# A head pair's attention handed to the scheduler in 16 stages instead of 8

## The chip, the core and the metric

The kernel runs on one core of a Trainium2 chip. The core has a matrix engine (TensorE, called PE in the profile, with its weight loads as PEld), a vector engine (VectorE, DVE), a scalar engine (ScalarE, ACT), GpSimd (POOL) and a queue that issues DMA transfers (SyncE, SP). Each engine works through its own instructions in the order of its queue and waits on semaphores for the others. The metric is the time of one execution on the device in microseconds (us); lower is better.

## The reference

The computation is a sliding-window attention followed by a feed-forward layer with softplus. There are 8 sequences of 576 tokens, 8 heads of 64 numbers each:

```python
scores = scale * np.matmul(q, k.transpose(0, 1, 3, 2))
mask = (rel >= 0) & (rel < window)              # window = 64
scores = np.where(mask, scores, -1000000000.0)
scores = scores - np.max(scores, axis=-1, keepdims=True)
attn = np.exp(scores)
attn = attn / (np.sum(attn, axis=-1, keepdims=True) + 1e-09)
x = np.matmul(attn, v)                          # then heads side by side: 4608 x 512
h = x @ w_in                                    # 512 x 2048
g = np.maximum(h, 0.0) + np.log1p(np.exp(-np.abs(h)))
out = g @ w_out                                 # 2048 x 512
```

All inputs are float32.

## The kernel before

**Blocks.** The 4608 tokens are cut into 12 blocks of 384. For each block the attention is computed for four head pairs, which gives x (512 rows by 384 tokens, as a high and a low part). Then come 16 steps of the feed-forward layer, one for each slice of 128 of the 2048 hidden columns. A step n consists of an *up* (12 matmuls into one bank of `ps_h`, line 396), a softplus, and a *down* (9 matmuls into the three banks of `ps_o`, line 417). Each product is taken in three passes, of high and low parts.

**Softplus.** For every step ScalarE reads the up's bank and takes the absolute value (line 400), the exponential (401) and the logarithm (402). VectorE reads the bank a last time and adds the maximum (404). A high part g0 is cast (406, on VectorE or ScalarE by turns) and a low part g1 subtracted (407, VectorE). The pool `ps_h` has two banks, so the up of step n+2 cannot start before line 404 of step n has run.

**Attention of a head pair** from the third block on: load q and k; split them into high and low parts (lines 242 to 247); three groups of score matmuls (262), each followed by a masked reading with row minimum on VectorE (269); the fold of the window (275); six exponentials (279); row sums and division (282 to 285); a split of the weights into three bf16 parts `nat` (304 to 311), which two transposing DMAs turn into `tr` (307, 312); a split of v (320 to 324); matmuls of `tr` with v (371), one group for each head; and the addition of the parts and the casts to x (376 to 380). The buffers `tr`, `nat`, `v_in`, `v12`, `v13`, `k0` and `k1` exist once.

**Order of the work.** `attention` is a generator; each `yield` ends a stage. Every stage, every up and every down is an event at a slot, and the events are emitted in the order of their slots:

```python
events.append((2 * n + 0.5, lambda g=g, f=f: ffn_up(g, f)))
events.append((2 * n + DOWN, lambda step=steps[n]: ffn_down(*step)))
```

With DOWN = 5.5 the down of step n stands behind the up of step n+2. A pair's stages stand at a base (8 slots apart from the next pair, so four feed-forward steps per pair) plus the numbers of `STG`; the third block has `BASE[2]` and `PACE[2]` for its base, and the table `STG2`. From slot 100 on (`PE_ORDERED_FROM`) TensorE keeps the order of the events. Before that slot on TensorE, and everywhere on the other engines, a scheduler orders the instructions of each engine by the order of emission and by a timeline of its own, so a stage's slot is a rank, not a time.

Of the kernel before, what the change touches and what calls it, by code (L numbers as in the profile page):

```python
# [8 lines left out]
F32 = mybir.dt.float32  # L9
BF16 = mybir.dt.bfloat16  # L10
F32R = mybir.dt.float32r
# [4 lines left out]
P = 128  # L16
TB = 384
# [3 lines left out]
CH = 64  # L21
NCH = TB // CH + 1
# [1 line left out]
SPLIT = 8  # L24
DOWN = 5.5
CONVERT = (-104, -98, -93, -88, -6, -3, 0, 3, 6, 8, 11, 13, 16, 18, 21, 24)
BASE = (-100, -10, 29)
PACE = (5, 4, 4.5)
STG0 = (-4.5, 0.5, 1, 2, 3, 4, 7, 8)
STG2 = (-6, -3, 0, 1, 2, 3, 12, 13)  # L30
STG = (-14, -8, 0, 1, 2, 3, 15, 17)
SH, SHP = -13, 8
PE_ORDERED_FROM = 100
MANUAL = {mybir.EngineType.PE}

# [4 lines left out]
def window_attention_softplus_ffn(  # L40
# [24 lines left out]
    nc = tc.nc  # L65
# [13 lines left out]
    att = ctx.enter_context(tc.tile_pool(name="att", bufs=1))  # L79
# [29 lines left out]
    W = CH + P  # L109
# [72 lines left out]
    def attention(g, hp):  # L182
        c0 = hp * P
        t0 = ORDER[g] * TB
        prev = t0 % S != 0
        by_pe = g < 2
        odd0 = g == 0 and hp % 2 == 1

        def bank():
            if not odd0:  # L190
                return ps_a.tile([P, 512], F32, name="ps_a")

            taken_ps[0] += 1
            return ps_o.tile([P, 512], F32, name=f"ps_o{taken_ps[0] % NJ}")

        heads = [slice(0, D), slice(D, P)]
# [9 lines left out]
        else:  # L206
            q_in = ld.tile([P, 2, TB], F32, name="q_in")
            k_in = ld.tile([P, 2, W - P + TB], F32, name="k_in")
            ts, ks = slice(t0, t0 + TB), slice(t0 - CH, t0 + TB)
# [9 lines left out]
        if by_pe:  # L219
            v_pad = v_pads[hp % 2]  # L220

            def load_v(rows, lay, j0, start):
                n = rows.stop - rows.start
                for j in range(j0, NJ):
                    dst = v_pad[rows, lay, j, :, :].rearrange("p h (i d) -> p (h i) d", i=2)[:, 0:4:3, :]
                    s = start + j * P
                    nc.sync.dma_start(dst, v[s : s + n, c0 : c0 + P].rearrange("p (h d) -> p h d", h=2))

            if t0 == 0:
                dst = v_pad[CH:P, 0, 0, :, :].rearrange("p h (i d) -> p (h i) d", i=2)[:, 0:4:3, :]  # L230
                nc.sync.dma_start(dst, v[0:CH, c0 : c0 + P].rearrange("p (h d) -> p h d", h=2))
            load_v(slice(0, P), 0, 1 if t0 == 0 else 0, t0 - CH)
            load_v(slice(0, CH), 1, 0, t0 + CH)
            load_v(slice(CH, P), 1, 0, t0)
        else:
            v_in = att.tile([P, NCH, P], F32, name="v_in")
            for half in heads:
                nc.sync.dma_start(v_in[half, :, :], v[ks, c0 : c0 + P].rearrange("(c p) n -> p c n", p=CH))
            q_hl = att.tile([P, 2, TB], F32R, name="q_hl")
            k_hi, k_lo = [att.tile([P, 2, W - P + TB], F32R, name=f"k{i}") for i in range(2)]  # L240
            low = heads[1]
            nc.scalar.copy(q_hl, q_in)  # L242
            nc.scalar.copy(k_hi, k_in)  # L243
            nc.vector.tensor_tensor(  # L244
                q_hl[low, :, :], q_in[low, :, :], q_hl[low, :, :].bitcast(F32), ALU.subtract
            )
            nc.vector.tensor_tensor(k_lo, k_in, k_hi.bitcast(F32), ALU.subtract)
        yield

# [26 lines left out]
        for hh in range(2):  # L276
            for j in range(NJ):
                i = hh * NJ + j
                nc.scalar.activation(  # L279
                    sv[:, i, 0:P], sv[:, i, 0:P], AF.Exp, bias=mn[:, hh, j : j + 1], scale=-1.0, accum_out=sm[:, i : i + 1]  # L280
                )
        nc.vector.tensor_scalar(sm, sm, 1.0e-9, None, ALU.add)
        nc.vector.reciprocal(sm, sm)
        pn = sv[:, :, 0:P]
        nc.vector.tensor_tensor(pn, pn, sm.unsqueeze(2).to_broadcast([P, 2 * NJ, P]), ALU.mult)  # L285
        if by_pe:

            pt = att.tile([P, 2, TB], F32, name="pt", tag="q_hl")
            for hh in range(2):
                pp = bank()  # L290
                for j in range(NJ):
                    tp(pp[:, j * P : (j + 1) * P], sv[:, hh * NJ + j, 0:P], ident)
                (nc.vector.tensor_copy if hh else nc.scalar.copy)(pt[:, hh, :], pp[:, :TB])
        else:

            nat = att.tile([P, 2, 4 * NJ, 2, CH], BF16, name="nat")
            tr = att.tile([P, 8 * NJ, P], BF16, name="tr")
            pv = [pn.rearrange("p i (f c) -> p i f c", f=2), nat.rearrange("p s (i f) b c -> p s i f b c", f=2)]

            def part(s, b):  # L300
                return pv[1][:, s, :, :, b, :]

            n = 4 * NJ
            nc.scalar.copy(part(0, 0), pv[0])
            nc.vector.tensor_tensor(pv[0], pv[0], part(0, 0), ALU.subtract)
            nc.scalar.copy(part(0, 1), pv[0])  # L306
            nc.sync.dma_start(
                tr[:, 0:n, :], nat[:, 0, :, :, :].rearrange("p n b c -> p (n b c)"), transpose=True
            )
            nc.vector.tensor_tensor(part(1, 0), pv[0], part(0, 1), ALU.subtract)  # L310
            nc.vector.tensor_copy(nat[:, 1, :, 1, :], nat[:, 0, :, 0, :])
            nc.sync.dma_start(
                tr[:, n:, :], nat[:, 1, :, :, :].rearrange("p n b c -> p (n b c)"), transpose=True
            )

            v12 = att.tile([P, NCH, 2, 2, D], BF16, name="v12")
            v13 = att.tile([P, NCH, 2, D], BF16, name="v13")
            vv = v_in.rearrange("p c (h d) -> p c h d", h=2)
            up, low = heads
            nc.scalar.copy(v12[:, :, :, 0, :], vv)  # L320
            nc.vector.tensor_tensor(vv, vv, v12[:, :, :, 0, :], ALU.subtract)  # L321
            nc.scalar.copy(v12[:, :, :, 1, :], vv)  # L322
            nc.vector.tensor_tensor(v13[low, :, :, :], vv[low, :, :, :], v12[low, :, :, 1, :], ALU.subtract)
            nc.vector.tensor_copy(v13[up, :, :, :], v12[up, :, :, 0, :])
# [13 lines left out]
        for hh in range(2):  # L338
# [14 lines left out]
            for s in range(2):  # L353
                for c in range(0 if prev else 1, NCH):
# [3 lines left out]
                    n = s * 4 * NJ + (hh * NJ + j) * 2  # L358
# [6 lines left out]
                    else:  # L365
                        at = n * P + CH
# [83 lines left out]
    for g in range(NB):  # L450
        for hp in range(NP):
            if g < 3:
                base = BASE[g] + PACE[g] * hp
            else:
                base = 2 * NF * (g - 1) + SHP * hp + SH
            stages = attention(g, hp)
            for at in STG if g >= 3 else STG2 if g >= 2 else STG0:
                events.append((base + at, lambda stages=stages: next(stages, None)))
    loaded = 0
    for n, (g, f, first, last) in enumerate(steps):  # L460
# [57 lines left out]
```

## Time and profile before

| | |
|---|---|
| Runs of the kernel before | 1089.43 us median of 3 (1089.07 to 1093.37) |
| The profiled execution's own time | 1091.76 us |
| Its span, first to last instruction | 1090.0 us |
| TensorE busy | 1011.9 us, 93% |
| VectorE busy | 826.5 us, 76% |
| ScalarE busy | 743.1 us, 68% |
| Mean granted TensorE clock | 0.977 |

The span has three parts: until about 137 us the first two blocks' attention and the preparation of the weights; then the feed-forward steps together with the attention of later blocks, until about 958 us; then the last steps without attention. Rows of the timeline read: start in us, duration in us, engine, line, operation, output and inputs, count of merged instructions, and in brackets the idle time before it with the engine that ended it.

### The profile page before, as it was taken

What the parts mean: (1) busy time and instruction counts of PE and PEld (TensorE: products, weight loads), DVE (VectorE), ACT (ScalarE), POOL (GpSimd) and SP (SyncE); (2) the same over time, 40 slices, a digit from 0 to 9 for tenths busy, and PEclk for the clock granted to TensorE, in tenths of its full rate; (3) what the DMA queues carried; (4) which work ended last, traced back from release to release, by engine and by line L of the source; (5) the groups of instructions that cost most, each with busy time, mean ns of one, the idle gap of its engine ahead of it and who ended that gap; (6) DMA issues with size and microseconds to landing.
All of it is one profiled execution on the core that took longest, in us unless ns stands there. A gap on an engine that the chain in (4) does not pass through costs nothing.

```text
span 1090.0 us, 16756 instructions
## 1 busy us (share of the span) xinstructions
PE 1011.9 (93%) x5888; PEld 882.7 (81%) x5888; DVE 826.5 (76%) x1797; ACT 743.1 (68%) x1705; POOL 53.4 (5%) x53
## 2 busy tenths in 40 slices
PE   5879689999999999999999999999999999999998
PEld 3667588887888888888887888888888888888897
DVE  7799897687878777887788778878877877875332
ACT  4466487776876776776777677667767766775433
POOL 3233420000000000000000000000000000000000
PEclk8889789999999999999999999999999999999999
DMA  6575254465645443543444344434535743521000
GB/s 196 159 248 186 80 144 111 92 144 99 161 92 117 107 102 78 136 125 79 121 111 108 107 107 122 111 83 113 143 78 95 156 89 79 143 57 29 29 1 30
DMA packets 209750, 119.07 MB, mean 109 GB/s; under 512 B 143361, under 2 KB 201729, under 8 KB 208129
## 3 DMA queue, kind: packets, MB, share of 16 engines
q1 hardware_dynamic: 209664, 118.00, 43.4%
q8 instruction: 46, 0.75, 0.3%
q14 instruction: 40, 0.32, 0.1%
HBM read 76.28 MB, written 10.22 MB: 79 GB/s over the span
## 4 chain that ended last, share of the span: by engine, by line
PE 58%; ACT 17%; DVE 16%; DMA 4%; issue 3%; SPq 1%; ACTq 0%
PE ps_h L396 25%; PE ps_o L417 23%; ACT st L279 6%; PE ps_a L371 6%; PE ps_a L262 4%; DVE st L285 3%; DVE v_in L321 3%; ACT k L243 2%; ACT q_hl L242 2%; DVE st L269 2%; DVE u L404 2%; ACT u L400 1%; ACT v L322 1%; ACT u L401 1%; ACT x L379 1%
## 5 line engine op out<-in xcount | busy, mean ns | idle before, releaser
L396 PE MATMUL ps_h<-x,w 128*128 128x384 f32 x2304 | 454.2, 345 | 41.6 <-DVE u L404 40.9
L396 PEld LDWEIGHTS ps_h<-x,w 128*128 128x128 f32 x2304 | 404.6, 190 | 69.2 <-DVE u L404 56.5
L417 PE MATMUL ps_o<-w,g 128*128 128x512 f32 x1728 | 433.3, 394 | 0.7 <-DVE g L407 0.7
L417 PEld LDWEIGHTS ps_o<-w,g 128*128 128x128 f32 x1728 | 316.7, 188 | 57.7 <-DVE g L407 1.1
L400 ACT ACTIVATE u<-ps_h 128x384 f32<-128x384 f32 x192 | 93.5, 487 | 143.0 <-PE ps_h L396 126.6
L404 DVE SCALAR_TENSOR_TENSOR u<-ps_h,u 128x384 f32<-128x384 f32 x192 | 106.1, 553 | 77.0 <-ACT u L402 76.0
L407 DVE TENSOR_TENSOR g<-u,g 128x384 fp32r<-128x384 f32 x192 | 105.6, 550 | 24.2 <-ACT g L406 22.6
L279 ACT ACTIVATE st<-st,mn 128x128 f32<-128x128 f32 x288 | 111.5, 391 | 14.1 <-DVE st L275 14.1
L402 ACT ACTIVATE u<-u 128x384 f32<-128x384 f32 x192 | 100.2, 522 | 4.4
L401 ACT ACTIVATE u<-u 128x384 f32<-128x384 f32 x192 | 100.7, 525 | 3.4
L269 DVE CUSTOM_DVE_ANT_0 st<-ps_a,mask 128x192 f32<-128x192 f32 x216 | 68.5, 354 | 43.7 <-PE ps_a L262 41.7
L406 ACT CAST g<-u 128x384 fp32r<-128x384 f32 x112 | 57.3, 511 | 40.5 <-DVE u L404 40.2
L371 PEld LDWEIGHTS <-v 128*128 128x128 bf16 (+1 forms) x1088 | 60.1, 104 | 30.0 <-issue 16.1
L371 PE MATMUL ps_a<-tr,v 128*64 128x128 bf16 (+2 forms) x1088 | 78.3, 215 | 0.0
L262 PE MATMUL ps_a<-k,q_hl 128*128 128x192 f32 x480 | 75.5, 281 | 0.0
L262 PEld LDWEIGHTS ps_a<-k,q_hl 128*128 128x128 f32 x480 | 68.8, 193 | 3.5 <-DVE q_hl L244 0.3
L322 ACT CAST v<-v_in 128x896 bf16<-128x896 f32 x40 | 37.5, 938 | 40.5 <-DVE v_in L321 40.5
L376 ACT COPY xf<-ps_a 64x384 f32<-64x384 f32 x80 | 38.2, 477 | 28.0 <-PE ps_a L371 27.0
L310 DVE TENSOR_TENSOR nat<-st,nat 128x768 bf16<-128x768 f32 x40 | 38.3, 957 | 23.7 <-ACT nat L306 23.7
L279 ACT ACTIVATION_READ_ACCUMULATOR st<-st,mn 128x1 f32 x288 | 54.5, 189 | 0.0
L285 DVE TENSOR_TENSOR st<-st,sm 128x768 f32<-128x768 f32 x48 | 50.2, 1047 | 1.3
L377 DVE TENSOR_TENSOR xf<-ps_a,xf 64x384 f32<-64x384 f32 x80 | 44.0, 550 | 5.8 <-ACT xf L376 3.6
(81 smaller groups left out, 893.7 us busy)
## 6 DMA issues: line engine op xcount, KB each, us to landing
k_in<-in_kT_dram SPq DMA_DIRECT2D x80, 224.0 KB, 4.0
v_in<-in_v_dram SPq DMA_DIRECT2D x80, 224.0 KB, 3.6
q_in<-in_qT_dram SPq DMA_DIRECT2D x84, 192.0 KB, 4.1
raws<-in_w_words_dram SPq DMA_DIRECT2D x12, 1024.0 KB, 5.8
out_dram<-raw SPq DMA_DIRECT2D x12, 512.0 KB, 3.0
raw<-in_w_words_dram SPq DMA_DIRECT2D x8, 512.0 KB, 5.0
out_dram<-raw SPq DMA_DIRECT2D x12, 256.0 KB, 2.7
v_pad<-in_v_dram SPq DMA_DIRECT2D x52, 32.0 KB, 2.4
```

The lines of the kernel that those rows point to most:

```text
L262: mm(spv[:, hh, :], q_hl[:, hh, js], part[:, hh, kc], start=(hh == 0 and i == 0), stop=(hh == 1 and i == 1), skip_group_check=True,)
L269: nc.vector.tensor_tensor_reduce(st[:, hh, j, :], spv[:, hh, :], m, QSCALE, 3.0e38, ALU.add, ALU.min, mn[:, hh, j : j + 1])
L279: nc.scalar.activation(sv[:, i, 0:P], sv[:, i, 0:P], AF.Exp, bias=mn[:, hh, j : j + 1], scale=-1.0, accum_out=sm[:, i : i + 1])
L285: nc.vector.tensor_tensor(pn, pn, sm.unsqueeze(2).to_broadcast([P, 2 * NJ, P]), ALU.mult)
L371: mm(av[: D if s else P, osl], v13[:, c, hh, :] if s else v12[:, c, hh, :, :], src, start=(i == 0), stop=(i == len(passes) - 1), skip_grou ...
L396: mm(hv, weight(0, a, f)[:, c * P : (c + 1) * P], x[b][c], start=(i_mm == 0), stop=(i_mm == 3 * NC - 1))
L400: nc.scalar.activation(u, hv, AF.Abs)
L401: nc.scalar.activation(u, u, AF.Exp, scale=-1.0)
L402: nc.scalar.activation(u, u, AF.Ln, bias=1.0)
L404: nc.vector.scalar_tensor_tensor(gf, hv, 0.0, u, ALU.max, ALU.add)
L407: nc.vector.tensor_tensor(gt[1], gf, gt[0].bitcast(F32), ALU.subtract)
L417: mm(ops[g][j], gt[a][:, js], weight(1, b, f), start=(first and i == 0), stop=(last and i == 2),)
```

## The change

The stages of a pair from the third block on are cut smaller, and their slots are set anew:

- The load of v moves from the stage that splits q and k to a stage of its own behind the transposes. In the stage table its slot goes from -8 to 7.1 of the pair's base. The split of v was in the stage at 3 and is now at 12 and 14.
- The split of q and that of k are stages of their own (at -5.9 and -5; both were at -8).
- The six exponentials are two stages of three (3 and 4), the sums and the division a third (5), the split of the weights two more (6 and 7). All of that was one stage at 3.
- The matmuls of `tr` with v move from 15 and 17 to 16 and 17.
- The base moves by one slot (SH from -13 to -12). The third block uses the same table; its base goes from 29 to 24 and its pairs stand 7 slots apart instead of 4.5.

No instruction is added or removed; each engine has the same instructions in another order. The diff, without hunks that only repeat a `yield`:

```diff
-BASE = (-100, -10, 29)
-PACE = (5, 4, 4.5)
+BASE = (-100, -10, 24)
+PACE = (5, 4, 7)
 STG0 = (-4.5, 0.5, 1, 2, 3, 4, 7, 8)
-STG2 = (-6, -3, 0, 1, 2, 3, 12, 13)
-STG = (-14, -8, 0, 1, 2, 3, 15, 17)
-SH, SHP = -13, 8
+STG = (-13, -5.9, -5, 0, 1, 2, 3, 4, 5, 6, 7, 7.1, 12, 14, 16, 17)
+SH, SHP = -12, 8
...
-            v_in = att.tile([P, NCH, P], F32, name="v_in")
-            for half in heads:
-                nc.sync.dma_start(v_in[half, :, :], v[ks, c0 : c0 + P].rearrange("(c p) n -> p c n", p=CH))
             q_hl = att.tile([P, 2, TB], F32R, name="q_hl")
-            k_hi, k_lo = [att.tile([P, 2, W - P + TB], F32R, name=f"k{i}") for i in range(2)]
             low = heads[1]
             nc.scalar.copy(q_hl, q_in)
-            nc.scalar.copy(k_hi, k_in)
...
+            yield
+            k_hi, k_lo = [att.tile([P, 2, W - P + TB], F32R, name=f"k{i}") for i in range(2)]
+            nc.scalar.copy(k_hi, k_in)
             nc.vector.tensor_tensor(k_lo, k_in, k_hi.bitcast(F32), ALU.subtract)
...
+            if not by_pe:
+                yield
         nc.vector.tensor_scalar(sm, sm, 1.0e-9, None, ALU.add)
...
             n = 4 * NJ
+            yield
             nc.scalar.copy(part(0, 0), pv[0])
             nc.vector.tensor_tensor(pv[0], pv[0], part(0, 0), ALU.subtract)
+            yield
             nc.scalar.copy(part(0, 1), pv[0])
...
+            yield
+            v_in = att.tile([P, NCH, P], F32, name="v_in")
+            for half in heads:
+                nc.sync.dma_start(v_in[half, :, :], v[ks, c0 : c0 + P].rearrange("(c p) n -> p c n", p=CH))
+            yield
...
-            for at in STG if g >= 3 else STG2 if g >= 2 else STG0:
+            for at in STG if g >= 2 else STG0:
```

**TensorE from slot 100 on.** Write V for a group of `tr`-v matmuls (an earlier pair's), S for a group of score matmuls, U for an up and D for a down. A pair's eight slots ran V U S D V S U S D U D U D before, and run V S U V S D S U D U D U D now. The counts are the same.

**ScalarE, around the six exponentials of a pair in a later block.** The rows are the instructions in the order of the queue; `u_6755` and `u_6825` are the softplus buffers of two steps that follow each other, `st` holds the scores, `xf` the attention's result. Before:

```order
L322 CAST v12_6576<-v_in_6229 128x14x64
L400 ACTIVATE u_6755<-ps_h_6742 128x384
L243 CAST k0_6701<-k_in_6543 128x896
L242 CAST q_hl_6700<-q_in_6542 128x768
L379 CAST x0_2_0_6645<-xf_6647 128x384
L401 ACTIVATE u_6755<-u_6755 128x384
L279 ACTIVATE st_6687,sm_6689<-st_6687,mn_6688 128x128 x6
L402 ACTIVATE u_6755<-u_6755 128x384
L400 ACTIVATE u_6825<-ps_h_6812 128x384
```

Now (lines 407, 408 and 409 are the softplus lines 400, 401 and 402 of before; 276 is 279, 386 is 379, 237 is 242):

```order
L329 CAST v12_6808<-v_in_6654 128x14x64
L243 CAST k0_6789<-k_in_6565 128x896
L237 CAST q_hl_6760<-q_in_6564 128x768
L386 CAST x0_2_0_6666<-xf_6668 128x384
L407 ACTIVATE u_6776<-ps_h_6763 128x384
L408 ACTIVATE u_6776<-u_6776 128x384
L276 ACTIVATE st_6686,sm_6688<-st_6686,mn_6687 128x128 x4
L409 ACTIVATE u_6776<-u_6776 128x384
L276 ACTIVATE st_6686,sm_6688<-st_6686,mn_6687 128x128 x2
L407 ACTIVATE u_6828<-ps_h_6815 128x384
```

The casts of k, q and x, which stood between the first and the second operation of a step's softplus, now stand ahead of its first; two of the six exponentials moved behind the logarithm (409).

**VectorE, the same stretch.** The first rows are the split of k and q and the cast of x, then come the row sums (282), their reciprocal (283), the division (285) and the last operations of the softplus. Before:

```order
L323 TENSOR_TENSOR v13_6577<-v_in_6229,v12_6576 64x896
L275 TENSOR_TENSOR st_6687<-st_6687 128x6x64
L247 TENSOR_TENSOR k1_6702<-k_in_6543,k0_6701 128x896
L244 TENSOR_TENSOR q_hl_6700<-q_in_6542,q_hl_6700 64x768
L380 TENSOR_TENSOR x1_2_0_6646<-xf_6647,x0_2_0_6645 128x384
L282 TENSOR_SCALAR sm_6689<-sm_6689 128x6
L283 RECIPROCAL sm_6689<-sm_6689 128x6
L285 TENSOR_TENSOR st_6687<-st_6687,sm_6689 128x6x128
L404 SCALAR_TENSOR_TENSOR u_6755<-ps_h_6742,u_6755 128x384
L406 CAST g0_6760<-u_6755 128x384
L404 SCALAR_TENSOR_TENSOR u_6825<-ps_h_6812,u_6825 128x384
L407 TENSOR_TENSOR g1_6761<-u_6755,g0_6760 128x384
```

Now (411, 413 and 414 are the lines 404, 406 and 407 of before; 244 is 247, 238 is 244, 387 is 380, 281 to 284 are 282 to 285; 266 is 269):

```order
L384 TENSOR_TENSOR xf_6668<-ps_a_6718,xf_6668 64x384
L411 SCALAR_TENSOR_TENSOR u_6709<-ps_h_6696,u_6709 128x384
...
L330 TENSOR_TENSOR v13_6809<-v_in_6654,v12_6808 64x896
L413 CAST g0_6714<-u_6709 128x384
L272 TENSOR_TENSOR st_6686<-st_6686 128x6x64
L244 TENSOR_TENSOR k1_6790<-k_in_6565,k0_6789 128x896
L238 TENSOR_TENSOR q_hl_6760<-q_in_6564,q_hl_6760 64x768
L387 TENSOR_TENSOR x1_2_0_6667<-xf_6668,x0_2_0_6666 128x384
L414 TENSOR_TENSOR g1_6715<-u_6709,g0_6714 128x384
L411 SCALAR_TENSOR_TENSOR u_6776<-ps_h_6763,u_6776 128x384
L281 TENSOR_SCALAR sm_6688<-sm_6688 128x6
...
L284 TENSOR_TENSOR st_6686<-st_6686,sm_6688 128x6x128
```

Line 411 of a step (`u_6776`) now stands ahead of the sums and the division instead of behind them. The step before it (`u_6709`) has its lines 411, 413 and 414 between the splits; before, no row of a softplus stood between 269 and 285 there.

**Start.** On TensorE the two orders are the same for the first 405 instructions, which reach to about 152 us in the trace of before; the third block's score matmuls are where they part.

More of the change, by code (lines that the diff above doesn't have):

```diff
@@ L321, in attention @@
             nc.vector.tensor_tensor(vv, vv, v12[:, :, :, 0, :], ALU.subtract)
+            yield
             nc.scalar.copy(v12[:, :, :, 1, :], vv)
```

## The prediction

> **What bounds the kernel now.** I read the page first: shares of the engines and the costliest groups.
>
> ```profile
> PE 1011.9 (93%) x5888; PEld 882.7 (81%) x5888; DVE 826.5 (76%) x1797; ACT 743.1 (68%) x1705; POOL 53.4 (5%) x53
> L396 PE MATMUL ps_h<-x,w 128*128 128x384 f32 x2304 | 454.2, 345 | 41.6 <-DVE u L404 40.9
> ```
>
> TensorE is busy 93% of the span, and nearly all idle time before its ups (41.6 us) is ended by VectorE's line 404, the last reading of a bank of `ps_h`. Then the busy time by stretches (columns: span, busy TensorE, weight loads, VectorE, ScalarE, GpSimd, then granted clock, DMA share, GB/s):
>
> ```profile
> 382.00:958.00 576.00, 547.44 (x3323) 480.04 (x3324) 459.21 (x1017) 418.91 (x955) 0.00 (x0) 1.00 0.45 108
> 958.00:1040.00 82.00, 82.00 (x472) 73.03 (x472) 41.89 (x85) 44.50 (x93) 0.00 (x0) 1.00 0.14 35
> 109.00:136.00 27.00, 16.23 (x85) 14.07 (x83) 24.09 (x39) 11.14 (x28) 12.59 (x8) 0.73 0.25 81
> ```
>
> Between 382 and 958 us TensorE is idle 576.00 - 547.44 = 28.56 us at full clock. After 958 us, without attention, it is never idle for 82 us, also at full clock. So a TensorE without gaps keeps its clock on this core, and what is to be had is that idle time. The timeline of TensorE has it in 28 equal pieces, one for each head pair, all before the same up. The first and the last:
>
> ```profile
> 382.46 2.38 PE L396 MATMUL ps_h<-x,w 128*128 128x384 f32 x12 [1.05 <-DVE u L404]
> ...
> 956.84 2.35 PE L396 MATMUL ps_h<-x,w 128*128 128x384 f32 x12 [1.04 <-DVE u L404]
> ```
>
> One pair in full:
>
> ```profile
> 514.72 0.91 PE L371 MATMUL ps_a<-tr,v 128*128 128x128 bf16 x12
> 515.55 2.35 PE L396 MATMUL ps_h<-x,w 128*128 128x384 f32 x12
> 517.75 0.59 PE L262 MATMUL ps_a<-k,q_hl 128*128 128x192 f32 x4
> 518.17 2.23 PE L417 MATMUL ps_o<-w,g 128*128 128x512 f32 x9
> 521.08 0.69 PE L262 MATMUL ps_a<-k,q_hl 128*128 128x192 f32 x4
> 521.60 2.29 PE L396 MATMUL ps_h<-x,w 128*128 128x384 f32 x12
> 523.73 0.59 PE L262 MATMUL ps_a<-k,q_hl 128*128 128x192 f32 x4
> 524.16 2.23 PE L417 MATMUL ps_o<-w,g 128*128 128x512 f32 x9
> 526.22 2.27 PE L396 MATMUL ps_h<-x,w 128*128 128x384 f32 x12
> 528.33 2.25 PE L417 MATMUL ps_o<-w,g 128*128 128x512 f32 x9
> 531.60 2.36 PE L396 MATMUL ps_h<-x,w 128*128 128x384 f32 x12 [1.02 <-DVE u L404]
> 533.79 2.25 PE L417 MATMUL ps_o<-w,g 128*128 128x512 f32 x9
> 535.88 0.91 PE L371 MATMUL ps_a<-tr,v 128*128 128x128 bf16 x12
> ```
>
> What makes the up at 531.60 late is the step whose up starts at 521.60 (same bank). Its softplus on ScalarE, and its end on VectorE:
>
> ```profile
> 524.45 0.49 ACT L400 ACTIVATE u<-ps_h 128x384 f32<-128x384 f32 x1
> 524.84 0.94 ACT L243 CAST k<-k_in 128x896 fp32r<-128x896 f32 x1
> 526.81 0.52 ACT L401 ACTIVATE u<-u 128x384 f32<-128x384 f32 x1
> 527.24 0.39 ACT L279 ACTIVATE st<-st,mn 128x128 f32<-128x128 f32 x1
> 529.55 0.51 ACT L402 ACTIVATE u<-u 128x384 f32<-128x384 f32 x1
> 533.99 0.49 ACT L400 ACTIVATE u<-ps_h 128x384 f32<-128x384 f32 x1 [1.04 <-PE ps_h L396]
> ```
>
> ```profile
> 521.80 0.36 DVE L269 CUSTOM_DVE_ANT_0 st<-ps_a,mask 128x192 f32<-128x192 f32 x1 [0.21 <-PE ps_a L262]
> 528.74 0.56 DVE L380 TENSOR_TENSOR x<-xf,x 128x384 fp32r<-128x384 f32 x1
> 530.12 0.96 DVE L285 TENSOR_TENSOR st<-st,sm 128x768 f32<-128x768 f32 x1
> 530.99 0.55 DVE L404 SCALAR_TENSOR_TENSOR u<-ps_h,u 128x384 f32<-128x384 f32 x1
> 531.58 0.36 DVE L406 CAST g<-u 128x384 fp32r<-128x384 f32 x1
> 532.32 0.55 DVE L407 TENSOR_TENSOR g<-u,g 128x384 fp32r<-128x384 f32 x1
> ```
>
> Line 400 starts at 524.45, but 401 only at 526.81: three casts, from 524.84 on, stand between. Line 402 starts at 529.55, behind all six exponentials that begin at 527.24. VectorE is then inside the division (285, from 530.12), and 404 runs from 530.99 to 531.54. The up starts 0.06 us later. ScalarE and VectorE are not full (418.91 and 459.21 of 576 us); it is the order of their queues that holds the bank.
>
> **The change, part by part.** No instruction is added, so every term is a wait.
>
> *The gap at the up.* Its price is read from starts. From a down to the next up it is 528.33 to 531.60, 3.27 us; without a gap 524.16 to 526.22, 2.06 us: 1.21 us more. The up behind the gap holds TensorE 2.19 us (to 533.79), the one at 526.22 only 2.11: 0.08 more. Together 1.29 us a pair, and 28 pairs make 36.1 us. The recorded idle of 28.56 us is smaller because the rows of matmuls overlap.
>
> The Trainium skill, "Perfetto Trace Analysis", section "Tensor Engine Instruction (MATMUL, LD_WEIGHTS)", says that the profiler computes a matmul's end from its size and does not observe it. The trace agrees: the down at 528.33 is shown to last 2.25 us, the one at 524.16 2.23, and the next starts after 2.06. By recorded idle the sum would be 28.56 instead of 36.1.
>
> *Does it vanish?* I take the new order of the queues and the durations above. Call the pair's ups x, y, z and w in TensorE's new order V S Ux V S D S Uy D Uz D Uw D. Up y plays the part of the step above, and Uw needs its bank. Line 400 starts 2.39 us after an up starts (531.60 to 533.99) if ScalarE is free, which has done the three casts while TensorE was still in y. Then come 0.5 for 400, 0.43 for 401 (526.81 to 527.24), four exponentials, 529.55 - 527.24 = 2.31 us for six, so 1.54, then 402 with 0.55: about 5.4 us after y's start. VectorE reaches 404 a little later, by its own queue: from the reading at 521.80 to the cast of x at 528.74 it now takes 6.94 us as before, and has 404 and 406 of x in addition (0.74 together: 531.58 to 532.32 holds one of each), then the cast of x (0.56 in its row, 0.47 where the next row overlaps it) and 407 (0.55): 8.70 us from the start of that reading, which is 0.72 after the second S starts (521.08 to 521.80). So 407 of x ends 9.42 us after that S, and 404 of y 0.5 later, at 9.9. TensorE goes from that S through D, S, Uy, D, Uz, D to Uw in 0.52 + 2.06 + 0.43 + 2.11 + 2.06 + 2.11 + 2.06 = 11.35 us (521.08 to 521.60 for the S behind a V, 523.73 to 524.16 for one behind other work). The bank is free 1.4 us early, where it was 1.21 late. Both S and V groups cost the same as before: one up less stands behind a V (2.20, from 515.55 to 517.75, against 2.11), one S more does (0.52 against 0.42).
>
> *What is late next.* The down behind Uz takes g1 of x. It starts 0.52 + 2.06 + 0.43 + 2.11 + 2.06 + 2.11 = 9.29 us after the S, when 407 of x ends at 9.42. But g1 enters only with the third of nine matmuls, 2 x 2.06 / 9 = 0.46 us later. So it is 0.3 early, too close to call. I bound the loss by 0 and 0.3 us a pair (0 to 8.4 us) and take 0.05 (1.4 us), since the rows sit on the early side. At a block's border Uz is the first up with the new x. Its eleventh matmul takes the low part of the last pair's x, which VectorE finishes when it begins 407 of x, at about 9.42 - 0.55 = 8.9 us; the up starts at 7.2 and reaches that matmul at 7.2 + 10 x 2.11 / 12 = 9.0. A few such borders at up to 0.3 us stay within the bound.
>
> *The loads.* On SP the load of v still follows the transposes, and both wait for the same things as before: the v buffer is free when 323 ends.
>
> ```profile
> 525.04 1.09 DVE L323 TENSOR_TENSOR v<-v_in,v 64x896 bf16<-64x896 f32 x1
> ```
>
> ```profile
> 526.16 1.29 SPq L238 DMA_DIRECT2D v_in<-in_v_dram  x2
> ```
>
> ```profile
> v_in<-in_v_dram SPq DMA_DIRECT2D x80, 224.0 KB, 3.6
> ```
>
> 323 starts at 525.04 and ends at 526.13, the load is issued at 526.16, takes 1.29 to issue and 3.6 to land, so is there at about 531. In the new order 323 ends some 5.4 us after the second S, and the next split of v is wanted half a V before the next second S, 19.9 - 0.4 - 5.4 = 14 us later: 9 us to spare. It costs nothing; the cover is the steps between.
>
> *The third block and the start.* TensorE's order is unchanged to 152 us, so I take no change there. Between 137 and 344 us TensorE now waits at these places, above all:
>
> ```profile
> 144.88 5.30 PE L396 MATMUL ps_h<-x,w 128*128 128x384 f32 x20 [2.67 <-DVE u L404]
> 246.83 0.96 PE L417 MATMUL ps_o<-w,g 128*128 128x512 f32 x3 [0.66 <-DVE g L407]
> 249.41 2.35 PE L396 MATMUL ps_h<-x,w 128*128 128x384 f32 x12 [1.62 <-DVE u L404]
> 343.64 2.35 PE L396 MATMUL ps_h<-x,w 128*128 128x384 f32 x12 [1.50 <-DVE u L404]
> ```
>
> Together 2.67 + 0.66 + 1.62 + 1.50 = 6.45 us. The third block's pairs start earlier and are spread more evenly, while the scheduler decides TensorE's order. No row of before shows the new order, so I bound it: all of the 6.45 gone, or one wait like the largest for each of the block's four pairs, 4 x 2.67 = 10.7 lost. Nearest is no change: the same instructions, the same two engines behind. I take 0.
>
> A long wait would cost more than itself: in the window from 109 to 136 us, where TensorE is busy 16.23 of 27 us, the clock is 0.73. The Trainium skill, "TensorE: Matmul & The Clock Gate", section "Part 1: The HAM clock gate (the \"warmup\" mystery)", puts the bound at an idle window of about 3.4 us; the gaps of 1 us leave the clock at 1.00 here, which agrees, so their removal gives no clock on top.
>
> *Sum.* 1090.0 - 36.1 + 1.4 = 1055.3 us of span, 34.7 less. The profiled execution took 1091.76 us, so 1057 by its own time; the median of the runs is 2.3 below that execution, and I forecast from it: 1089.43 - 34.7 = 1054.7, rounded to 1055.
>
> **Rivals.** *The wait moves to the down.* The slack of 0.3 us is worked from single rows; if VectorE's chain is 0.9 longer, 0.6 us a pair stay: 1055 + 17 = 1072. For it: VectorE has the least slack of all. Against: its steps are taken from the same rows in the same order. Chance 0.13.
>
> *The third block pays.* Its attention now comes ahead of more of the feed-forward work and VectorE is dense there; the 10.7 us above, or twice that with the clock: 1066 to 1076. Chance 0.09.
>
> *Slower: v comes late.* Its load moved from 11 slots ahead of the split to 5. If the transposes in front of it on SP are held for longer than the 9 us to spare, ScalarE's split of v stands in its queue ahead of x's softplus and VectorE's behind it; each us then falls on the down, which has 0.3. From 1.6 us of lateness on nothing is gained (0.3 + 1.29); at 3.5, 1055 + 28 x 3.2 = 1145. Against: issue and landing are as in the rows above. Chance 0.05.
>
> *It does nothing.* The scheduler might keep the old order; the rows of the queues show that it does not. VectorE could become the bound: 459.21 / 576 of 21.2 us is 16.9 us a pair, against 19.9 us of TensorE. With part gained and part lost it ends near 1089. Chance 0.05.
>
> **How the numbers follow.** Forecast 0.68, the rest as above. Faster by more than 0.5% (5.4 us, about what a measurement of this kernel can tell): forecast and the first two rivals, 0.90; slower 0.05; same 0.05. The range goes from 1055 - 6.5 - 1.4 = 1047 to the first rival and the bulk of the second, 1074. That leaves out the last two rivals (0.10) and about 0.1 of the others.
>
> **What would show it.** Right: between some 350 and 930 us TensorE's idle time falls from 28.6 to below 4 us, no row of an up waits for VectorE there, the pair takes 19.9 us instead of 21.2, and clock stays 1.00. If the slack was misjudged, rows of downs (now line 424) wait for VectorE's 414. If v is late, ScalarE waits for the DMA into `v_in`. If the third block pays, new gaps stand between 152 and 344 us. The forecast is wrong if the gap before one up per pair stays, or if it returns before another row.

## The result, and the profile after

The changed kernel takes 1060.39 us (median, 1057.45 to 1065.32); timed beside it, the kernel before took 1091.08 us. The ratio is 0.9723 with a 95% interval of 0.9678 to 0.9767. The profiled execution took 1059.67 us with a span of 1057.9, so 32.1 us less than the span of before (1090.0). The forecast was 1055, the range 1047 to 1074.

The page of the changed kernel, engines and the costliest group (line 403 is the up, 411 the last reading of its bank):

```profile
PE 1004.5 (95%) x5888; PEld 883.0 (83%) x5888; DVE 813.9 (77%) x1797; ACT 740.2 (70%) x1705; POOL 54.4 (5%) x53
L403 PE MATMUL ps_h<-x,w 128*128 128x384 f32 x2304 | 448.9, 342 | 9.4 <-DVE u L411 8.3
```

The idle time before the ups fell from 41.6 to 9.4 us. Where it went is seen by stretches. First the kernel before, then the changed one (columns as above: span, busy TensorE, weight loads, VectorE, ScalarE, GpSimd, clock, DMA share, GB/s):

```profile
152.00:344.00 192.00, 187.93 (x1140) 163.58 (x1139) 152.49 (x341) 146.80 (x336) 2.83 (x2) 1.00 0.53 115
382.00:930.00 548.00, 521.53 (x3171) 457.41 (x3172) 435.26 (x967) 396.60 (x899) 0.00 (x0) 1.00 0.45 108
```

```profile
152.00:344.00 192.00, 186.42 (x1116) 161.80 (x1115) 149.87 (x333) 143.50 (x331) 1.93 (x2) 1.00 0.48 114
382.00:930.00 548.00, 548.00 (x3348) 487.32 (x3347) 450.87 (x1025) 421.01 (x971) 0.00 (x0) 1.00 0.49 115
```

In the later blocks TensorE has no idle time left. Before it lacked 26.47 us there. Between 152 and 344 us it got a little worse: 5.58 us idle against 4.07. One pair of the changed kernel on TensorE, from one V to the same V of the next pair (line 259 is S, 378 is V, 424 the down):

```profile
511.92 0.91 PE L378 MATMUL ps_a<-tr,v 128*128 128x128 bf16 x12
512.76 0.69 PE L259 MATMUL ps_a<-k,q_hl 128*128 128x192 f32 x4
513.29 2.27 PE L403 MATMUL ps_h<-x,w 128*128 128x384 f32 x12
515.40 0.91 PE L378 MATMUL ps_a<-tr,v 128*128 128x128 bf16 x12
516.24 0.69 PE L259 MATMUL ps_a<-k,q_hl 128*128 128x192 f32 x4
516.77 2.25 PE L424 MATMUL ps_o<-w,g 128*128 128x512 f32 x9
518.86 0.59 PE L259 MATMUL ps_a<-k,q_hl 128*128 128x192 f32 x4
519.28 2.29 PE L403 MATMUL ps_h<-x,w 128*128 128x384 f32 x12
521.41 2.24 PE L424 MATMUL ps_o<-w,g 128*128 128x512 f32 x9
523.49 2.27 PE L403 MATMUL ps_h<-x,w 128*128 128x384 f32 x12
525.60 2.24 PE L424 MATMUL ps_o<-w,g 128*128 128x512 f32 x9
527.68 2.27 PE L403 MATMUL ps_h<-x,w 128*128 128x384 f32 x12
529.78 2.25 PE L424 MATMUL ps_o<-w,g 128*128 128x512 f32 x9
531.87 0.91 PE L378 MATMUL ps_a<-tr,v 128*128 128x128 bf16 x12
```

No row has a bracket. The pair takes 531.87 - 511.92 = 19.95 us; before it was 535.88 - 514.72 = 21.16. On ScalarE and VectorE the same stretch reads:

```profile
519.50 0.94 ACT L243 CAST k<-k_in 128x896 fp32r<-128x896 f32 x1
520.34 0.83 ACT L237 CAST q_hl<-q_in 128x768 fp32r<-128x768 f32 x1
521.07 0.51 ACT L386 CAST x<-xf 128x384 fp32r<-128x384 f32 x1
521.61 0.49 ACT L407 ACTIVATE u<-ps_h 128x384 f32<-128x384 f32 x1
522.13 0.53 ACT L408 ACTIVATE u<-u 128x384 f32<-128x384 f32 x1
```

```profile
516.97 0.36 DVE L266 CUSTOM_DVE_ANT_0 st<-ps_a,mask 128x192 f32<-128x192 f32 x1 [1.91 <-PE ps_a L259]
525.11 0.55 DVE L414 TENSOR_TENSOR g<-u,g 128x384 fp32r<-128x384 f32 x1
525.58 0.55 DVE L411 SCALAR_TENSOR_TENSOR u<-ps_h,u 128x384 f32<-128x384 f32 x1
```

The third S of the pair (518.86) now comes ahead of the up (519.28) and not behind it. The cast of k begins at 519.50, when that S is over (518.86 + 0.59 = 519.45), so ScalarE does its three casts while TensorE is in the up, and the softplus's first operation (407, at 521.61) follows the up at once. Before, it was the casts that came after that operation. The bank is read for the last time at 525.58 + 0.55 = 526.13; the up that needs it starts at 527.68.

What got worse stands between 286 and 303 us, in the third block:

```profile
286.30 1.66 PE L424 MATMUL ps_o<-w,g 128*128 128x512 f32 x6 [0.92 <-ACT g L413]
288.51 0.51 PE L378 MATMUL ps_a<-tr,v 128*128 128x64 bf16 x7 [0.55 <-DMA tr<-nat]
293.38 0.84 PE L378 MATMUL ps_a<-tr,v 128*64 128x64 bf16 x14 [2.72 <-DMA tr<-nat]
303.02 1.67 PE L424 MATMUL ps_o<-w,g 128*128 128x512 f32 x6 [1.14 <-ACT g L413]
```

The gaps of before at 246.83, 249.41 and 343.64 are gone, but two waits for the transposing DMA (3.27 us) and two for ScalarE have come: TensorE reaches V before `tr` has landed.

To price stretches without the modelled ends of matmuls I take the start of the n-th step's first softplus operation on ScalarE (line 400 of before) and subtract. Steps 8 to 56 hold the third block, steps 56 to 164 are 27 pairs of later blocks. The last three columns are experiments that are told below (E10: the base slot alone; E11: the change with the third block's old places; E12: a third bank alone):

| | before | the change | E10 | E11 | E12 |
|---|---|---|---|---|---|
| step 8 at | 139.97 | 138.67 | 140.49 | 140.10 | 148.28 |
| steps 8 to 56 | 244.91 | 246.53 | 242.28 | 242.11 | 231.83 |
| steps 56 to 164 | 574.34 | 541.95 | 541.76 | 541.95 | 540.43 |

So 27 pairs gained 32.39 us, 1.20 each, the stretch to step 8 gained 1.3, and the steps 8 to 56 lost 1.6. Together that is the 32.1 us.

### The profile page after: what moved, and what is told of

Its sections match the earlier page's. It is cut to its first block, busy times and chain, and to the rows that moved or that the text cites. A ratio compares the mean times of both kernels' runs of the same rounds, so it can differ in the third digit from the quotient of the medians.

```text
span 1057.9 us, 16725 instructions
## 1 busy us (share of the span) xinstructions
PE 1004.5 (95%) x5888; PEld 883.0 (83%) x5888; DVE 813.9 (77%) x1797; ACT 740.2 (70%) x1705; POOL 54.4 (5%) x53
## 4 chain that ended last, share of the span: by engine, by line
PE 83%; DVE 10%; DMA 4%; ACT 1%; issue 1%; SPq 1%; ACTq 0%
PE ps_h L403 35%; PE ps_o L424 35%; PE ps_a L378 6%; PE ps_a L259 6%; DVE st L266 1%; DMA raws<-in_w_words_dram 1%; DVE ws L171 1%; DVE ws L170 1%; DVE st L284 1%; DMA v_in<-in_v_dram 1%; DVE ws L169 1%; DMA tr<-nat 1%; DMA kbd<-in_kT_dram 1%; DMA raw<-in_w_words_dram 1%; DVE ws L168 1%
## 5 line engine op out<-in xcount | busy, mean ns | idle before, releaser
L403 PE MATMUL ps_h<-x,w 128*128 128x384 f32 x2304 | 448.9, 342 | 9.4 <-DVE u L411 8.3
L378 PE MATMUL ps_a<-tr,v 128*64 128x128 bf16 (+3 forms) x1088 | 78.8, 215 | 3.3 <-DMA tr<-nat 3.3
L259 PE MATMUL ps_a<-k,q_hl 128*128 128x192 f32 x480 | 78.8, 288 | 0.0
L307 ACT CAST nat<-st 128x768 bf16<-128x768 f32 x40 | 33.2, 831 | 38.3 <-DVE st L305 38.2
L327 DVE TENSOR_TENSOR v_in<-v_in,v 128x896 f32<-128x896 f32 x40 | 43.5, 1087 | 4.5 <-ACT v L326 4.5
```

The source lines that it names most:

```text
L259: mm(spv[:, hh, :], q_hl[:, hh, js], part[:, hh, kc], start=(hh == 0 and i == 0), stop=(hh == 1 and i == 1), skip_group_check=True,)
L378: mm(av[: D if s else P, osl], v13[:, c, hh, :] if s else v12[:, c, hh, :, :], src, start=(i == 0), stop=(i == len(passes) - 1), skip_grou ...
L403: mm(hv, weight(0, a, f)[:, c * P : (c + 1) * P], x[b][c], start=(i_mm == 0), stop=(i_mm == 3 * NC - 1))
```

## The experiments

**Which part of the change makes the gain.** The change does three things from the third block on: finer stages, other slots for TensorE's groups, another place for the third block. E1 takes the kernel before and sets only the slots, E2 the change without them.

```diff
E1, against the kernel before
-STG = (-14, -8, 0, 1, 2, 3, 15, 17)
-SH, SHP = -13, 8
+STG = (-14, -8, 0, 1, 2, 3, 16, 17)
+SH, SHP = -12, 8
E2, against the change
-STG = (-13, -5.9, -5, 0, 1, 2, 3, 4, 5, 6, 7, 7.1, 12, 14, 16, 17)
-SH, SHP = -12, 8
+STG = (-13, -5.9, -5, 0, 1, 2, 3, 4, 5, 6, 7, 7.1, 12, 14, 15, 17)
+SH, SHP = -13, 8
```

> The kernel before with its 8 stages and its early load of v; only the slots of the matmuls move: the base by one slot (SH -13 to -12) and the first tr-v group from 15 to 16. Theory A, the finer stages make the gain: the gap before one up per pair stays, about 1090 us. Theory B, the place of the score and tr-v groups between the ups and downs makes it, since on every engine the order of the queues in a later block becomes that of the change: about 1058 us, TensorE without idle time from some 380 to 930 us, a pair 19.95 us.

> The changed kernel with all 16 stages and the third block's new places, but the matmuls at the old slots (SH -13, first tr-v group at 15). Theory A: about 1058 us. Theory B: the gap of about 1.05 us before one up per pair is back, a pair takes 21.2 us, about 1090 us.

E1: 1055.0 us (ratio 0.9663, 0.962 to 0.9705). E2: 1092.52 us (ratio 1.002, 0.9999 to 1.0041). The windows of the later blocks, E1 first, then E2:

```profile
382.00:930.00 548.00, 548.00 (x3360) 487.26 (x3359) 449.37 (x1024) 419.22 (x959) 0.00 (x0) 1.00 0.48 113
```

```profile
382.00:930.00 548.00, 520.99 (x3169) 456.96 (x3170) 435.51 (x968) 396.37 (x899) 0.00 (x0) 1.00 0.45 108
```

The sixteen stages by themselves give nothing in the later blocks (steps 56 to 164 take 574.30 us in E2 and 574.34 before), and the eight stages with the new slots give all of it. ScalarE in E2 shows why:

```profile
503.74 0.49 ACT L407 ACTIVATE u<-ps_h 128x384 f32<-128x384 f32 x1
504.13 0.94 ACT L243 CAST k<-k_in 128x896 fp32r<-128x896 f32 x1
506.11 0.53 ACT L408 ACTIVATE u<-u 128x384 f32<-128x384 f32 x1
```

Although the casts are stages of their own, they stand behind the first operation of the softplus, as before, and the exponential comes 2.37 us after it. The gap before one up a pair is back:

```profile
510.89 2.35 PE L403 MATMUL ps_h<-x,w 128*128 128x384 f32 x12 [1.05 <-DVE u L411]
```

Two slots were set in E1. E5 sets the base alone (SH -12, all else as before), E6 the V slot alone (16 for 15).

> The kernel before with one number changed: the base moves by one slot (SH -13 to -12), so the score groups stand ahead of ups instead of downs and a down, not an up, follows the second of them. If the order of the score groups against the ups and downs decides, the whole gain is there: 1055 us within 5, a pair 19.9 to 20.0 us, no wait before an up from 380 to 930 us. If the later slot of the tr-v group (16) is needed, the gap of 1.05 us stays in every pair: about 1090 us.

> The kernel before with the other number changed alone: the first tr-v group goes from slot 15 to 16, the base stays. ScalarE's queue keeps the three casts and all six exponentials inside one step's softplus. If the base decides, the gap before one up per pair stays, 1088 to 1093 us; if the slot of the group decides, about 1055 us.

E5: 1054.2 us (ratio 0.9664, 0.963 to 0.9698). E6: 1093.06 us (ratio 1.0012, 0.9993 to 1.0032), with 26 waits of an up still there:

```profile
PE ps_h L396 <- DVE u L404: 27.1, 26, 1.1
```

The base alone it is. One slot more puts the first and the third group S ahead of an up, where they stood ahead of a down; with the second it is the other way round. The third S of a pair in E5 and the up behind it, and then ScalarE:

```profile
513.23 0.59 PE L262 MATMUL ps_a<-k,q_hl 128*128 128x192 f32 x4
513.65 2.29 PE L396 MATMUL ps_h<-x,w 128*128 128x384 f32 x12
```

```profile
513.87 0.94 ACT L243 CAST k<-k_in 128x896 fp32r<-128x896 f32 x1
515.98 0.49 ACT L400 ACTIVATE u<-ps_h 128x384 f32<-128x384 f32 x1
```

That is the order of the changed kernel, from a kernel with eight stages. In the kernel the split of k writes a buffer that exists once and that the third S reads, so it cannot start before that S is over. Where that S stands behind the up (before, E2, E6), the casts stand inside the softplus and the gap is there; where it stands ahead of it (the change, E1, E5), they stand in front, and the gap is gone. Two things are not shown by this. The base moves all stages of a pair, and that it is the third S and no other stage which places the casts is read from the code. And the casts do not move alone: in E5, as in the change, two of the six exponentials also come behind the logarithm, and the last reading of the bank comes ahead of the division; their shares were not tried apart.

**Whether it is the bank.** If a bank read too late is the whole cause, a third bank for `ps_h` must remove the wait with the old order untouched. E3 takes it from the attention's pool; E7 is E1 with the same banks.

```diff
-    ps_a = ctx.enter_context(tc.tile_pool(name="ps_a", bufs=3, space=bass.MemoryType.PSUM))
-    ps_h = ctx.enter_context(tc.tile_pool(name="ps_h", bufs=2, space=bass.MemoryType.PSUM))
+    ps_a = ctx.enter_context(tc.tile_pool(name="ps_a", bufs=2, space=bass.MemoryType.PSUM))
+    ps_h = ctx.enter_context(tc.tile_pool(name="ps_h", bufs=3, space=bass.MemoryType.PSUM))
```

> The kernel before with three banks for the ups (ps_h) and two for the attention (ps_a) instead of two and three; the queues' order in a later block stays. If it is the bank held by a late softplus that stops TensorE, the wait before the up goes (28 x 1.21 us) and part of it comes back as a wait of the third score group for its bank, up to 0.6 us a pair: 1057 to 1075 us. If ScalarE's or VectorE's work as such is the limit, the gap stays in another place and the time is about 1090 us.

> The matmul slots of the first experiment and three banks for the ups together. Both take away the same wait, so if that wait is all, the later blocks gain nothing over either alone (a pair 19.95 us) and only the start can differ: 1047 to 1057 us. If the third score group now waits for its bank (two for the attention), up to 0.6 us a pair are lost: up to 1072 us.

E3: 1052.11 us (ratio 0.9635, 0.9604 to 0.9666). E7: 1055.17 us (ratio 0.9662, 0.9629 to 0.9695). Windows of E3, then ScalarE in one of its pairs:

```profile
152.00:344.00 192.00, 192.00 (x1165) 171.34 (x1164) 152.09 (x340) 147.60 (x350) 0.00 (x0) 1.00 0.49 116
382.00:930.00 548.00, 548.00 (x3371) 485.68 (x3370) 459.01 (x1029) 421.63 (x959) 0.00 (x0) 1.00 0.49 114
```

```profile
510.21 0.94 ACT L243 CAST k<-k_in 128x896 fp32r<-128x896 f32 x1
512.19 0.52 ACT L401 ACTIVATE u<-u 128x384 f32<-128x384 f32 x1
```

ScalarE still has the casts in front of the softplus's exponential (401), 1.98 us after the first of them began, and nobody waits for the bank. The last reading of that step's bank (404) is as late as before, 9.40 us after its up starts at 506.97 (before 530.99 - 521.60 = 9.39), and the up after the next one starts ahead of it:

```profile
515.78 2.27 PE L396 MATMUL ps_h<-x,w 128*128 128x384 f32 x12
516.37 0.55 DVE L404 SCALAR_TENSOR_TENSOR u<-ps_h,u 128x384 f32<-128x384 f32 x1
```

With two banks that up would have had to wait until 516.37 + 0.55 = 516.92, about 1.14 us. The bank was the cause. The Trainium skill, "Perfetto Trace Analysis", section "Optimization Strategy", says that a gap which repeats on the engine that should be full can mean too little PSUM for the next tile. That holds here: one bank more takes 26.5 us of recorded idle time to zero. But an order that reads the bank earlier (E5) does it with two banks as well.

The bank has a price at the start: with two banks for the attention, step 8 comes 5.1 us (E3) and 8.3 us (E7) later than before. The wait of the third group of scores for a bank, which I had feared, does not come in the later blocks. E7 is no better than E1 (1055.17 and 1055.0 us): its steps 56 to 164 take 541.88 us and those of E1 541.91, so where the order has already taken the wait away the bank adds nothing there, and step 56 comes 2.0 us later.

**What the third block's new places cost.** E4 is the change with the third block's base and pace (29 and 4.5) and its stage table as before; only the load of v stays behind the transposes.

```diff
-BASE = (-100, -10, 24)
-PACE = (5, 4, 7)
+BASE = (-100, -10, 29)
+PACE = (5, 4, 4.5)
+STG2 = (-6, -3, -3, 0, 1, 2, 3, 3, 3, 3, 3, 3, 3, 3, 12, 13)
-            for at in STG if g >= 2 else STG0:
+            for at in STG if g >= 3 else STG2 if g >= 2 else STG0:
```

> The changed kernel with the third block's attention at its old places (base 29, pairs 4.5 slots apart, old slots within the pair). Later blocks are as in the change. The time should be that of the change within 4 us; if the new places cost the waits between 286 and 304 us (5.3 us idle in the trace of the change), it is up to 5 us faster, if they avoided worse, slower.

E4: 1056.66 us (ratio 0.9671, 0.9639 to 0.9704), and between 152 and 344 us TensorE idles 1.42 us instead of 5.58:

```profile
152.00:344.00 192.00, 190.58 (x1133) 166.38 (x1133) 149.91 (x337) 145.94 (x337) 3.08 (x2) 1.00 0.48 115
```

The interval overlaps that of the change, so four of the kernels were timed side by side: the change (E9), the base slot alone (E10), E4's kernel (E11) and the third bank alone (E12).

> The change itself, timed side by side with three other versions on one chip. Both theories: about 1060 us, as first measured (1060.39).

> The kernel before with only the base slot moved by one (SH -12), beside the change on the same chip. Theory A (the base slot makes the whole gain, the third block's new places cost some 5 us): about 1054, 5 to 6 below the change, interval clear of it. Theory B (the third block's new places cost nothing, the difference between the two was chip to chip): within 2 us of the change.

> The change with only the third block's old places, beside the change on the same chip. Theory A: about 1056, 4 below the change. Theory B: within 2 us of it.

> The kernel before with only a third bank for the up projection's result (and one fewer for the attention's), beside the others. If the bank alone is the best of the versions: about 1052, some 2 below the base slot alone and 8 below the change. If its start, 5 us slower in the first look, decides, it ends level with the base slot alone, 1054.

| | median, us | lowest to highest | ratio to before | interval |
|---|---|---|---|---|
| E9, the change | 1061.09 | 1060.26 to 1062.42 | 0.9723 | 0.9706 to 0.9739 |
| E10, base slot alone | 1056.62 | 1055.05 to 1057.89 | 0.968 | 0.9663 to 0.9697 |
| E11, third block's old places | 1056.13 | 1054.01 to 1058.07 | 0.9676 | 0.9656 to 0.9695 |
| E12, third bank alone | 1052.61 | 1052.05 to 1053.22 | 0.9644 | 0.9628 to 0.9659 |

The intervals of E10 and E11 lie below that of the change: the new places cost 4.5 to 5 us. By the starts of steps it is 246.53 - 242.11 = 4.4 us in the third block. The waits of TensorE between 152 and 344 us, the change first, then E11:

```profile
PE ps_a L378 <- DMA tr<-nat: 3.3, 2, 2.7
PE ps_o L424 <- ACT g L413: 2.1, 2, 1.1
```

```profile
PE ps_h L404 <- DVE u L412: 1.6, 1, 1.6
```

E12 is 4 us below E10 and 8.5 below the change, with one number changed in each of two lines. Its step 8 comes 8.3 us later, but by step 56 it is 4.8 us ahead of the kernel before (380.1 against 384.9), and the later blocks take 1.5 us less than in the change. Which of base, pace and stage table makes the third block's loss was not tried apart.

**How much slack the new order has.** E8 puts three copies into VectorE's queue per pair.

```diff
+            nc.vector.tensor_copy(v13[up, :, :, :], v12[up, :, :, 0, :])
+            nc.vector.tensor_copy(v13[up, :, :, :], v12[up, :, :, 0, :])
+            nc.vector.tensor_copy(v13[up, :, :, :], v12[up, :, :, 0, :])
```

> The changed kernel with three more copies of the high part of v (0.38 us each) on VectorE for each pair, work that the output does not need; two of them stand between the reading of the second score group and the low part of g of the step that the down takes. The prediction puts the slack of that down at 0.3 us, the trace of the change at 0.4. Then 2 x 0.28 to 2 x 0.41 us of additional work make TensorE wait 0.15 to 0.5 us a pair before or within that down (4 to 18 us in the whole); with a slack of over 0.8 us nothing changes.

One execution: 1066.83 us, span 1065.1. On TensorE the down behind Uz, and VectorE's operation that it needs (line numbers are three higher: 427 is the down, 417 the low part g1):

```profile
524.33 2.59 PE L427 MATMUL ps_o<-w,g 128*128 128x512 f32 x9
526.76 2.27 PE L406 MATMUL ps_h<-x,w 128*128 128x384 f32 x12
```

```profile
524.43 0.55 DVE L417 TENSOR_TENSOR g<-u,g 128x384 fp32r<-128x384 f32 x1
```

The second S of this pair starts at 514.97, so g1 is there after 524.98 - 514.97 = 10.01 us instead of 9.42: two of the copies stand in front of it. The next up comes 2.43 us after the down instead of 2.08, 0.35 more. So in this pair 0.59 us late costs 0.35, and the slack is 0.24. The wait stands inside the down and not ahead of it, hence only with the weight loads:

```profile
PEld ps_o L427 <- DVE g L417: 9.8, 19, 0.5
PE ps_h L406 <- DVE x L390: 2.9, 7, 0.4
```

Steps 56 to 164 took 552.94 us, 11.0 more than in the change, 0.41 a pair. At seven block borders an up waits as well, for the low part of x.

## Why the prediction was right, and where not

- **The gap at the up** vanishes in all pairs, as forecast, and from the cause named: the bank is read for the last time earlier, because the queues of ScalarE and VectorE have another order. E2, E5 and E6 show that this order makes it, E3 that the bank does. How much the casts, the two exponentials and the division each give stays open.
- **Its price.** The term of 1.29 us a pair was 0.09 too high. The 1.21 from the starts of down and up is right. The up behind the gap did get shorter (2.19 to 2.10), but most of this was given back by the downs, which take 2.08 to 2.09 us each in the changed pair (521.41 to 523.49, 529.78 to 531.87), where I had taken 2.06. Measured: 1.20, so 28 pairs give 33.6 us, not 36.1. To price by starts was right in the main: for 27 pairs it gives 32.7 by 1.21, the trace 32.4, and the recorded idle time would have given 27.5.
- **When the bank comes free.** 411 of y was worked out to end 9.9 us after the second S. It ends at 526.13 - 516.24 = 9.89. Uw starts 11.44 us after that S, not 11.35.
- **The down behind Uz.** 414 of x was put at 9.42 and ends at 525.66 - 516.24 = 9.42; the down starts at 9.36, before it, and is not held up, since g1 enters with the third matmul. The 0.05 us a pair (1.4 us) taken for it is 0. The slack of 0.3 was 0.24 by E8, and E8 also shows the border wait of the working. The rival that the wait moves to the down did not come, but it was as near as I had said.
- **The load of v and the clock.** As forecast: no wait of TensorE in the later blocks, and the clock is 1.00 with the 1 us gaps and without them.
- **The third block and the start**, taken as 0, within -6.45 and 10.7: the start gained 1.3 (step 8 begins between 137.3 and 141.6 us in the kernels whose attention keeps three banks, so this is scatter) and the third block lost 2.8, the 1.6 between steps 8 and 56 and the 1.2 that the first of the 28 pairs, which lies there, had gained. This is the mechanism of the second rival, new gaps between 152 and 344 us, at a quarter of its price. The doubling by the clock that the rival allowed for did not come: with waits of up to 2.72 us the clock of this stretch is 1.00. Which wait comes was not foreseen: not VectorE, but the transposing DMA.
- **The sum.** 33.6 + 1.3 - 2.8 = 32.1 us, against 34.7. That they lie so close is in part luck: the third block's 2.8 was made up by scatter (1.3) and by a loss at the down that was allowed for and did not come (1.4). Of the 5.7 us by which the median lies above 1054.7, the forecast before it was rounded, this is 2.6; 1.7 are the kernel before, which came at 1091.08 beside the change and not at 1089.43; the rest is between the profiled executions and the medians.
- **What the working passed over.** It took the order of all queues as given by the change as a whole, and never asked which edit gives it. The experiments answer: one slot in the base. The stages that the change is named after do nothing to the time, and the third block's new places, put at zero, cost 4.5 to 5 us against its old places under the new base. Had the edits been costed one by one, the base slot would have carried the whole term and the third block would have stood apart, with a sign to look for.

## What to carry to other kernels

When a bank is read late, list what stands between the operations that free it in each in-order queue, and what lets those intruders start; here three casts, two exponentials and a division came out of the way when one slot put a group of matmuls ahead of an up instead of behind it, for more than 3% of the time. Before cutting stages finer, try the coarse ones one slot to either side, and one bank more: both smaller edits were faster than the change. Check each part of a bundle apart: one part gave 35 to 37 us, one nothing, and one took 4.5 to 5 back.

## What was not expected of the hardware

- A down shown as one row can hide a wait: in E8 it lasts 2.59 us instead of 2.24 with no idle time in front, and only the weight loads' waits name the cause.
- The granted clock between 137 and 152 us is not a property of the kernel: the change shows 0.62 in its first profile and 0.82 in that of E9, with the same instructions, and step 56 starts within 0.7 us (385.20 and 385.83). The two windows:

```profile
137.00:152.00 15.00, 12.22 (x52) 11.69 (x51) 13.40 (x34) 12.39 (x33) 4.24 (x3) 0.62 0.57 166
```

```profile
137.00:152.00 15.00, 11.76 (x57) 11.06 (x56) 13.50 (x34) 11.99 (x31) 4.67 (x3) 0.82 0.54 152
```
